# A sliding-window attention and SiLU feed-forward kernel: another order of loads, v of two batches by the hardware queue, attention half a tile further ahead

## The chip, the cores and the metric

The kernel runs on one core of a Trainium2 chip. A core has a matrix engine (PE, with its weight loads shown as PEld), a vector engine (DVE), a scalar engine with activation tables (ACT), a general engine (POOL) and a queue processor (SP); each works through its own instructions in the order in which they stand in the program, and they wait for each other by semaphores. Transfers are issued by SP (hardware queue) or POOL (software queue, which can change the type on the way) and run on 16 DMA engines. The metric is device time in microseconds, the median of three executions.

## The reference

```python
B, H, S, D = 8, 8, 576, 64                       # batch, heads, positions, head size
scores = q @ k.T / sqrt(D), kept where 0 <= i - j < 64
attn   = exp(scores - max) / (sum + 1e-9)
x      = (attn @ v), heads side by side          # 4608 tokens x 512
h      = x @ w_in                                # 512 x 2048
out    = (h * sigmoid(h)) @ w_out                # 2048 x 512
```

All inputs and the output are fp32; the kernel computes in bf16 with fp32 accumulation.

## The kernel before

**Blocks and tiles.** A batch has nine blocks of 64 positions; the 72 blocks run through all batches, and eight of them make a tile of 512 tokens, nine tiles in all. A block needs its own keys and the block before. The heads are worked on in two quads of four (a = 0, 1). For each quad of a group of blocks (`visit`): PE scores into four banks of PSUM (L339), ACT's exponential into `es` (L346), a multiplication with the mask on DVE (L353), PE values (L361) with a column of ones beside v for the sums, the reciprocal (L371) and the normalisation (L374) into `o` on DVE, and two DVE transposes (L380) into the tile's `xt`, of which there are three.

**Attention ahead.** Tile 0 is visited in groups of 3, 3 and 2 blocks as batch 0 arrives, tile 1 in two groups of four, and every later tile j + 1 as a whole, both quads, during the second layer of tile j, after its second product (`order[1]`).

**The two layers.** Tiles 0 and 1 run the first layer plain: 128x128 pieces of `w_in_sb` against 128 to 256 tokens (L388), and SiLU on ACT (L399) into `g`. Tile 0 runs the second layer plain too: 64 matmuls of 512 columns (L402). From tile 2 on the first layer, and from tile 1 on the second, use seven products in place of eight (`fast_first`, `fast_second`): 112 matmuls of 256 columns each (L438, L450). The sums of operands that this needs are made on DVE: `wsum1` and `wsum2` once, `xsum` from the tile's tokens (L411), `gsum` from the hidden activations (L407). Products are joined by copies of banks on ACT (L454) and additions on DVE (L457).

**Loads.** Batch 0 comes as fp32 by SP: k and q in thirds of 192 positions of a quad (`load_third`, L265) into memory that `gsum` and `wsum1` use later, v in four pieces and a half (L279, L276) into that of `wsum2`; casts (L291) and placements (`place_v`, L322) on ACT or DVE make bf16 of them. A piece of v needs three placements (`own`, `up`, `low`), as a block's values use a window of 128 positions that starts in the block before. POOL loads the rest with a change to bf16: w_in in eight pieces of 128 KB and four of 256 KB, batch 1 by thirds, w_out in eight pieces of 256 KB, the later batches by heads (`load_head`, L269). DVE transposes thirds with L298/L301 and heads with L308/L311, three operations each. `place_all` makes the `up` and `low` copies of the later batches on DVE (L327, L329).

**The order.** `Plan` simulates the engines with a cost for each operation, picks the ready operation with the lowest priority number, and writes the program in that order. Dependencies given to it decide its order alone; the waits in the program come from the data that instructions share. So an operation that the plan places late has no wait of its own unless it shares data with what it follows.

Of the kernel before, what the change touches and what calls it, by code (L numbers as in the profile page):

```python
# [31 lines left out]
class Plan:  # L32


    LATE = {"PE": 0.06, "ACT": 0.15, "DVE": 0.12, "POOL": 0.15, "SP": 0.0}
# [55 lines left out]
    def run(self):  # L91
# [3 lines left out]
        table, pipe = "exp", 0.0  # L95
# [7 lines left out]
        while left:  # L103
# [3 lines left out]
            while events and events[0] <= now + 1e-9:  # L107
                heapq.heappop(events)
            while self.returns and self.returns[0][0] <= now + 1e-9:
                _, _, b = heapq.heappop(self.returns)  # L110
                self.owner[b.idx], self.free_at[b.idx] = None, b.till
                if b.unit is not None:
                    b.unit.held -= 1
            moved = True
            while moved:
# [5 lines left out]
                for e in engines:  # L121
# [22 lines left out]
                    if op["dma"] is None:  # L144
                        op["seen"] = end + self.LATE[e]
                    else:
                        begin = max(pipe, end + 1.2)
                        pipe = begin + op["dma"]
                        op["seen"] = pipe + 2.0
# [4 lines left out]
                    for u, lat in op["users"]:  # L154
                        same = e in u["us"] and len(u["us"]) == 1 and op["dma"] is None
# [9 lines left out]
        self.order, self.span = order, max(op["seen"] for op in order)  # L165
# [5 lines left out]
def kernel(ctx, tc, q, k, v, w_in, w_out, out):  # L171
# [7 lines left out]
    NQ = 2  # L179
    NXT = 3  # L180
    NGP = 10
    scale = 1.0 / float(D) ** 0.5
# [18 lines left out]
    qT = [keep.tile([128, 6, 2, 96, 2], BF16, name=f"qT{a}") for a in range(NQ)]  # L201
# [71 lines left out]
    def load_v(e, b, g):  # L273
        if g == 4:
            dst = stage_v8 if b == 0 else vv[b % 2][64:128, :, 8, 0:D]
# [17 lines left out]
    def turn_third(b, a, kk, i):  # L293
# [5 lines left out]
        else:  # L299
            dst = qT[a][:, n].rearrange("x t y z -> x (t y z)").bitcast(FP32).rearrange("x (t p c) -> x c t p", t=2, c=3)  # L300
            nc.vector.transpose(out=dst, in_=src.rearrange("x (c t w) -> x c t w", c=3, t=2))  # L301

    def turn_blocks(b, a, kk, i):
        src = nats[b % 2][a][kk][:, 384 * i:384 * i + 384].bitcast(FP32).rearrange("x (n t w) -> x n t w", n=3, t=2)
        n = 3 * (b % 2) + i
        if kk:
            dst = kT[a][:, 64 + 192 * n:256 + 192 * n].rearrange("x t y -> x (t y)").bitcast(FP32)
            nc.vector.transpose(out=dst.rearrange("x (n p t) -> x n t p", n=3, t=2), in_=src)  # L308
        else:
            dst = qT[a][:, n].rearrange("x t y z -> x (t y z)").bitcast(FP32)  # L310
            nc.vector.transpose(out=dst.rearrange("x (t n p) -> x n t p", t=2, n=3), in_=src)  # L311

    def place_v(e, b, what, g):
# [5 lines left out]
        else:  # L319
            whole = stage_vp[:, g] if b == 0 else t[:, :, 2 * g + 1, 0:D]  # L320
# [12 lines left out]
    def scores(bank, a, blocks):  # L333
        for x, nb in enumerate(blocks):
            n, s = nb % 18, (nb % 18) * 64
            for par in range(2):
                for h in range(4):
# [4 lines left out]
                        rhs=qT[a][r, n // 3, :, 32 * (n % 3):32 * (n % 3) + 32, par],  # L342
# [34 lines left out]
    def turn_out(a, z, nb, n):  # L377
        src = osb[a][:, 0:n].rearrange("k n d t -> k n (d t)").bitcast(FP32)[:, :, 32 * z:32 * z + 32]
        j, s = nb // 8, nb % 8 * 64
        nc.vector.transpose(out=xts[j % NXT][:, 2 * a + z, s:s + 64 * n].bitcast(FP32), in_=src)  # L380
# [87 lines left out]
    SOFT = 0.85  # L468
# [4 lines left out]
    def turn_plan(b, a, kk, i, deps, prio, whole):  # L473
        old = score_ops.get((b - 2, a), []) + ([c_k] if kk and b == 0 and i == 0 else [])
        op = p.add({"DVE": dve(192)}, lambda _: (turn_third if whole else turn_blocks)(b, a, kk, i), deps + old, prio, tag="turn")
        turned.setdefault((b, a, i), []).append(op)
# [6 lines left out]
    n_soft = [0]  # L483

    def soft(us, fn, deps=(), dma=0.0, tag="load", after=()):
        n_soft[0] += 1
        return p.add({"POOL": us}, fn, deps, n_soft[0], dma=dma, tag=tag, after=after)
# [3 lines left out]
    def hard(fn, deps=(), dma=0.0, tag="load"):  # L491
# [3 lines left out]
    win, wout = {}, []  # L495

    def load_first(i):
        for a in range(NQ):
            for kk in (1, 0):
                ld = hard(lambda e, a=a, kk=kk: load_third(e, 0, a, kk, i), dma=0.52)  # L500
                ca = p.add({"ACT": act(384), "DVE": dve(384)}, lambda e, a=a, kk=kk: cast_third(e, a, kk, i), [ld], -50 + i, tag="cast")
                cast_ops.append(ca)
                turn_plan(0, a, kk, i, [ca], -50 + i, True)

    def load_first_v(g):
        ld = hard(lambda e: load_v(e, 0, g), dma=1.15 if g < 4 else 0.58)
        if g == 4:
            placed[(0, 8)] = [place_plan(0, "last", 4, [ld, c_v[0]], -30 + g)] + placed.get((0, 8), [])
            cast_ops.extend(placed[(0, 8)])
            return  # L510
        own, up, low = [place_plan(0, w, g, [ld, c_v[0]], -30 + g) for w in ("own", "up", "low")]
        cast_ops.extend((own, up, low))
        placed.setdefault((0, 2 * g + 1), []).append(own)
        placed.setdefault((0, 2 * g), []).append(up)
        placed.setdefault((0, 2 * g + 2), []).append(low)

    def load_rows(b, thirds, prio):
        for i in thirds:
            for a in range(NQ):
                for kk in (1, 0):  # L520
                    ld = soft(SOFT, lambda e, a=a, kk=kk, i=i: load_third(e, b, a, kk, i), turn_ops.get((b - 2, a, kk), []), dma=0.63)
                    turn_plan(b, a, kk, i, [ld], prio + 0.1 * i, True)

    def load_heads(b, prio):
        for a in range(NQ):
            for kk in (1, 0):
                ld = [soft(SOFT, lambda e, a=a, kk=kk, h=h: load_head(e, b, a, kk, h), turn_ops.get((b - 2, a, kk), []), dma=0.72)
                      for h in range(4)]
                for i in range(3):
# [347 lines left out]
```

## Time and profile before

| | |
|---|---|
| runs | 341.97, 342.42, 343.35 us; median 342.42 |
| profiled execution | 341.61 us; span of its instructions 339.9 us |
| mean granted clock of PE | 0.936 of full speed |
| busy, share of the span | PE 85%, PEld 67%, DVE 69%, ACT 61%, POOL 33% |
| DMA | 88061 packets, 30.25 MB: 16.63 MB by POOL's queue, 12.98 MB by SP's |
| matmuls | 4416 |

The profile shows one execution, in us from the start of the span. Its chain of waits is followed back from the last instruction, at each step to what released it or to the instruction before it on its engine. Groups give busy time, mean ns of one, then the idle time before them and what ended it. In a timeline row, the bracket is the engine's idle time before the row and its releaser. Where records overlap in time, as matmuls do, the time of a group is its covered time.

### The profile page before, as it was taken

The page shows a single profiled execution, that of the slowest core. Times are in us where ns is not written, and L with a number is a line of the kernel's source. Part 1 is how long each engine was busy: PE and PEld are TensorE (multiplying, and loading weights), DVE is VectorE, ACT ScalarE, POOL GpSimd, SP SyncE. Part 2 cuts the span into 40 slices and gives each one's busy share as a digit, 9 for nine tenths or more (in the row PEclk, how much of TensorE's full clock was granted, in tenths as well). Part 3 has the DMA queues.
Part 4 walks back from the last instruction along what each step waited for, and adds up shares of the span by engine and source line. Part 5 has one row for each costly group of instructions (what it writes and reads, how often), then busy time and mean ns, then how long its engine had stood idle before and what let it go on. Part 6 is the DMA issues. An engine that isn't in the chain of part 4 may idle for free.

```text
span 339.9 us, 10402 instructions
## 1 busy us (share of the span) xinstructions
PE 289.0 (85%) x4416; PEld 226.8 (67%) x4422; DVE 233.8 (69%) x603; ACT 208.8 (61%) x386; POOL 110.7 (33%) x170
## 2 busy tenths in 40 slices
PE   8374217999979679996999999999979989999994
PEld 3132206954758558884887788788858877887883
DVE  2132253859654798988598889969978686967840
ACT  2141627960985548863885797396659648866931
POOL 7041424597792457197009450300030000000000
PEclk9967556999999989998999999999999999999998
DMA  5988998999995399499209990560090030003003
GB/s 82 164 138 145 138 188 118 116 136 119 195 125 53 35 193 101 46 92 223 25 2 101 182 86 4 88 94 2 4 177 3 2 113 17 0 4 125 2 0 123
DMA packets 88061, 30.25 MB, mean 89 GB/s; under 512 B 76752, under 2 KB 82896, under 8 KB 88016
## 3 DMA queue, kind: packets, MB, share of 16 engines
q0 software_dynamic: 76848, 16.63, 53.5%
q1 hardware_dynamic: 11168, 12.98, 11.9%
q8 instruction: 34, 0.56, 0.7%
q14 instruction: 11, 0.09, 0.1%
HBM read 36.70 MB, written 9.44 MB: 136 GB/s over the span
## 4 chain that ended last, share of the span: by engine, by line
PE 46%; DVE 23%; SPq 11%; ACT 8%; DMA 5%; issue 4%; POOL 1%; DVEq 0%; ACTq 0%
PE bank L438 22%; PE bank L450 15%; SPq L265 7%; DVE o L374 5%; PE bank L388 5%; DMA wsum<-in_v_dram 4%; SPq L279 4%; DVE es L353 3%; PE bank L402 3%; DVE gsum L407 3%; DVE xt L380 2%; ACT es L346 2%; ACT L346 2%; PE bank L339 2%; DVE kT L308 1%
## 5 line engine op out<-in xcount | busy, mean ns | idle before, releaser
L450 PEld LDWEIGHTS <-gsum 128*128 128x128 bf16 x512 | 47.6, 98 | 11.1 <-DVE gsum L407 3.5
L460 ACT ACTIVATE g<-bank 128x512 bf16<-128x512 f32 x84 | 48.7, 617 | 4.6 <-PE bank L438 3.6
L438 PEld LDWEIGHTS <-wsum 128*128 128x128 bf16 x448 | 44.5, 99 | 10.5 <-issue 2.6
L450 PE MATMUL bank<-wsum,gsum 128*128 128x256 bf16 x384 | 47.3, 273 | 2.8 <-DVE gsum L407 2.0
L438 PE MATMUL bank<-xsum,wsum 128*128 128x256 bf16 x336 | 46.5, 279 | 1.2 <-DVE xsum L411 1.0
L279 POOL DMA_DIRECT2D vv<-in_v_dram x28 | 25.5, 930 | 58.6 <-PE bank L361 50.0
L346 ACT ACTIVATE es<-bank 128x512 bf16<-128x512 f32 (+3 forms) x96 | 39.5, 496 | 6.0 <-PE bank L339 5.9
L438 PEld LDWEIGHTS <-w_in_sb 128*128 128x128 bf16 x336 | 32.9, 99 | 13.8 <-issue 7.1
L450 PEld LDWEIGHTS <-g 128*128 128x128 bf16 x384 | 36.6, 98 | 7.2 <-issue 2.3
L269 POOL DMA_DIRECT2D nat<-in_k_dram x48 | 28.8, 614 | 36.7 <-DVE qT L311 30.9
L454 ACT COPY ot<-bank 128x512 f32<-128x512 f32 x23 | 13.4, 591 | 44.2 <-PE bank L450 29.8
L438 PE MATMUL bank<-xt,w_in_sb 128*128 128x256 bf16 x224 | 32.7, 281 | 6.5 <-DVE xt L380 3.6
L457 DVE TENSOR_TENSOR bank<-bank,part 128x512 f32<-128x512 f32 x36 | 24.5, 695 | 19.9 <-ACT part L454 10.3
L450 PE MATMUL bank<-w_out_sb,g 128*128 128x256 bf16 x256 | 33.9, 273 | 2.2 <-ACT bank L454 2.1
L407 DVE TENSOR_TENSOR gsum<-g 128x512 bf16<-128x512 bf16 x64 | 26.9, 421 | 11.2 <-ACT g L460 7.1
L388 PE MATMUL bank<-xt,w_in_sb 128*128 128x192 bf16 (+2 forms) x320 | 33.3, 266 | 0.6 <-ACT es L346 0.6
L353 DVE TENSOR_TENSOR es<-es,strip 128x1024 bf16<-128x1024 bf16 (+3 forms) x48 | 25.4, 546 | 11.5 <-ACT es L346 10.8
L269 POOL DMA_DIRECT2D nat<-in_q_dram x48 | 29.3, 627 | 12.1 <-DVE qT L311 10.1
L339 PE MATMUL bank<-qT,kT 32*128 32x64 bf16 x1152 | 14.3, 194 | 21.8 <-DVE qT L301 17.4
L388 PEld LDWEIGHTS <-w_in_sb 128*128 128x128 bf16 x320 | 28.5, 103 | 4.1 <-issue 1.5
L454 ACT COPY part<-bank 128x512 f32<-128x512 f32 x36 | 20.7, 594 | 16.4 <-PE bank L450 16.3
L374 DVE TENSOR_TENSOR o<-bank,rc 128x384 bf16<-128x384 f32 (+2 forms) x56 | 29.4, 527 | 1.9
(64 smaller groups left out, 435.2 us busy)
## 6 DMA issues: line engine op xcount, KB each, us to landing
out_dram<-ot SPq DMA_DIRECT2D x18, 512.0 KB
vv<-in_v_dram POOLq DMA_DIRECT2D x28, 128.0 KB, 4.0
nat<-in_k_dram POOLq DMA_DIRECT2D x48, 72.0 KB, 2.9
nat<-in_q_dram POOLq DMA_DIRECT2D x48, 72.0 KB, 3.0
w_out_sb<-in_moe_w_out_dram POOLq DMA_DIRECT2D x8, 256.0 KB, 14.0
wsum<-in_k_dram SPq DMA_DIRECT2D x6, 192.0 KB
gsum<-in_q_dram SPq DMA_DIRECT2D x6, 192.0 KB
w_in_sb<-in_moe_w_in_dram POOLq DMA_DIRECT2D x8, 128.0 KB, 16.2
```

The costliest lines, as they stand in the source:

```text
L269: queue[e].dma_start(out=nats[b % 2][a][kk][32 * h:32 * h + 32].rearrange("p (n x) -> p n x", n=NB), in_=(q, k)[kk][b, 4 * a + h].rearrang ...
L279: queue[e].dma_start(out=dst, in_=v[b, :, 128 * g:128 * g + 128].rearrange("h p d -> p h d"))
L346: nc.scalar.activation(out=es[a][:, h, 0:64 * n], in_=banks[bank.idx][:, 0:64 * n], func=ACTF.Exp, scale=scale)
L353: nc.vector.tensor_mul(t, t, strip[:, s:s + n].rearrange("k n i -> k (n i)").unsqueeze(1).to_broadcast([128, 2, 64 * n]))
L374: nc.vector.tensor_mul(osb[a][:, x0:x0 + n].rearrange("k n d t -> k n t d"), at_values(bank, n)[:, :, :, 0:D], rcs[w][:, 0:n].unsqueeze(3) ...
L388: nc.tensor.matmul(banks[bank.idx][:, i * n:i * n + n], lhsT=w_in_sb[:, c, 128 * ft:128 * ft + 128], rhs=xts[j % NXT][:, c, lo:hi], start= ...
L407: (nc.vector.tensor_sub if i else nc.vector.tensor_add)(out=dst[i], in0=a, in1=b)
L438: nc.tensor.matmul(banks[bank.idx][:, 256 * i:256 * i + 256], lhsT=lhs(z, i), rhs=rhs(z), start=(start and i == 0 and z == 0), stop=(z == ...
L450: nc.tensor.matmul(banks[bank.idx][:, 256 * m:256 * m + 256], lhsT=lhs(m, i), rhs=rhs(i), start=(start and i == 0 and m == 0), stop=(stop ...
L454: copies[e](out=dst, in_=src)
L457: nc.vector.tensor_add(out=dst, in0=bank, in1=part)
L460: nc.scalar.activation(out=g_tile(pair, 256 * t, 256 * t + 256), in_=src.rearrange("k (f t) -> k f t", f=2), func=ACTF.Silu)
```

## The change

It alters the planner's picture of DMA (two lanes, one per queue, that share time packet by packet), several of its costs, and:

- w_in comes in sixteen pieces of 128 KB, each given a dependency on the sixth load of SP (`GATE = 5`); POOL's first fifty loads are planned strictly one after the other;
- v of batch 1 comes by SP as fp32, like batch 0's (`HARDV = 2`), behind the eighth load of POOL in the plan (`VGATE = 7`) and behind the placements of batch 0 that free the memory; POOL issues w_out directly behind the first third of batch 1;
- batches 2 and 3 are loaded by thirds (`ROWS = 3`), and a batch loaded by heads is transposed in one operation for each of k and q of a quad, with `qT` laid out anew;
- the `up` and `low` copies of v of batch 2 and later run on ACT (`VACT = 2`);
- the two transposes into `xt` become one;
- `visit` takes one quad or both. During the second layer of tile j now come quad 1 of tile j + 1 and quad 0 of tile j + 2 (in tile 1: both quads of tile 2 and quad 0 of tile 3), behind the first product (`order[0]`) instead of the second;
- tile 1's second layer is plain, with its four groups of 128 tokens one after the other; the fast second layer begins with tile 2 (`F2 = 2`).

```diff
-        dst = stage_vp[:, g] if b == 0 else vv[b % 2][:, :, 2 * g + 1, 0:D]
+        dst = stage_vp[:, g] if b < HARDV else vv[b % 2][:, :, 2 * g + 1, 0:D]
...
-    def turn_blocks(b, a, kk, i):
-        src = nats[b % 2][a][kk][:, 384 * i:384 * i + 384].bitcast(FP32).rearrange("x (n t w) -> x n t w", n=3, t=2)
+    def turn_blocks(b, a, kk):
+        src = nats[b % 2][a][kk].bitcast(FP32).rearrange("x (n t w) -> x n t w", n=NB, t=2)
...
-    def turn_out(a, z, nb, n):
-        src = osb[a][:, 0:n].rearrange("k n d t -> k n (d t)").bitcast(FP32)[:, :, 32 * z:32 * z + 32]
+    def turn_out(a, nb, n):
+        src = osb[a][:, 0:n].rearrange("k n d t -> k n (d t)").bitcast(FP32).rearrange("k n (z w) -> k n z w", z=2)
         j, s = nb // 8, nb % 8 * 64
-        nc.vector.transpose(out=xts[j % NXT][:, 2 * a + z, s:s + 64 * n].bitcast(FP32), in_=src)
+        dst = xts[j % NXT][:, 2 * a:2 * a + 2, s:s + 64 * n].bitcast(FP32)
+        nc.vector.transpose(out=dst.rearrange("x z (n p) -> x n z p", n=n), in_=src)
...
+    def load_hard_v(b, g, deps=()):
+        ld = hard(lambda e: load_v(e, b, g), list(deps) + stage_free.get(g, []), dma=("h256", 1024 if g < 4 else 512))
+        first_loads.append(ld)
+        names = ("own", "up", "low") if g < 4 else ("last",)
+        ops = [place_plan(b, w, g, [ld, c_v[b % 2]], -30 + 50 * b + g) for w in names]
...
-        up = p.add({"DVE": dve(n, 3000)}, lambda e: place_all(e, b, "up", g0, g1), lv, prio, tag="place")
+        us = {"ACT": act(n)} if b >= VACT else {"DVE": dve(n, 3000)}
+        up = p.add(us, lambda e: place_all(e, b, "up", g0, g1), lv, prio, tag="place")
...
-        for f in range(16):
-            for m in range(4):
+        for f, m in [(f, m) for f in range(16) for m in range(4)] if j == 0 else [(f, m) for m in range(4) for f in range(16)]:
...
-                    cp = p.add({"ACT": act(512), "DVE": dve(512)}, lambda e, m=m: fork(e, ot[:, m], banks[bank[m].idx]), [op], base + 5, give=[bank[m]], tag="out")
+                    cp = p.add({"ACT": act(512), "DVE": dve(512)}, lambda e, m=m: fork(e, ot[:, m], banks[bank[m].idx]), [op] + ot_free.get((m // 2, 0), []), base + 5, give=[bank[m]], tag="out")
...
-    for pi0, pi1 in ((0, 2), (2, 4), (4, 8)):
+    for pi0, pi1 in ((0, 2), (2, 4), (4, 6), (6, 8)):
         for c in range(4):
-            ld = soft(SOFT, lambda e, c=c, pi0=pi0, pi1=pi1: load_w_in(e, c, 256 * pi0, 256 * pi1), dma=0.39 * (pi1 - pi0))
+            ld = soft(SOFT, lambda e, c=c, pi0=pi0, pi1=pi1: load_w_in(e, c, 256 * pi0, 256 * pi1), [first_loads[GATE]], dma=("s1024", 64 * (pi1 - pi0)))
...
     load_rows(1, (0,), 20)
-    load_pairs(1, (0, 1))
+    for g in range(5):
+        load_hard_v(1, g, [soft_last[VGATE]])
...
+            if n_b[0] <= ROWS:
+                load_rows(n_b[0], (0, 1, 2), 100 * j - 80)
+            else:
+                load_heads(n_b[0], 100 * j - 80)
...
-        order = fast_second(j, j == NT - 1)
-        if j + 1 < NT:
-            visit(list(range(8 * j + 8, 8 * j + 16)), 100 * j + 52, after=[order[1]], sprio=100 * j + 50.0)
+        order = fast_second(j, j == NT - 1) if j >= F2 else plain_second(j)
+        todo = [(j + 1, 0)] * (j == 1) + [(j + 1, 1), (j + 2, 0)]
+        for i, (t, a) in enumerate(todo):
+            if t < NT:
+                load_until(8 * t + 7, j)
+                visit(list(range(8 * t, 8 * t + 8)), 100 * j + 52 + i, after=[order[0]], sprio=100 * j + 50.0 + 0.1 * i, quads=(a,))
```

More of the change, by code (lines that the diff above doesn't have):

```diff
@@ L164, in run @@
                     heapq.heappush(events, end)
-        self.order, self.span = order, max(op["seen"] for op in order)
+            next_flow()
+        self.order, self.span = order, max(op["seen"] or 0.0 for op in order)
         for op in order:
@@ L555, with visit @@
     n_val = [0]
-    def visit(blocks, prio, after=(), sprio=None):
+    def visit(blocks, prio, after=(), sprio=None, quads=(0, 1)):
         n, j = len(blocks), blocks[0] // 8
         exps, outs = [], []
-        for a in range(NQ):
-            bank = [Bank("start") for _ in range(4)]
+        for a in quads:
+            bank = [Bank("start" if n == 8 else "part") for _ in range(4)]
             need = []
@@ L566, in visit @@
                         need += turned[(x // NB, a, x % NB // 3)]
-            sc = p.add({"PE": 0.1 + 0.12 * n}, lambda _, bank=bank, a=a: scores(bank, a, blocks), need, prio + 0.01 * a if sprio is None else sprio + 0.01 * a,
+            sc = p.add({"PE": 0.1 + 0.08 * n}, lambda _, bank=bank, a=a: scores(bank, a, blocks), need, prio + 0.01 * a if sprio is None else sprio + 0.01 * a,
                        take=bank, after=after, tag="scores")
@@ L583, in visit @@
                     need = need + placed[divmod(nb, NB)]
-                va = p.add({"PE": 0.1 + 0.1 * m}, lambda _, vb=vb, a=a, part=part, x0=x0: values(vb, a, part, x0), need, (prio if sprio is None else sprio) + 0.01 * a + 0.001 * x0,
+                va = p.add({"PE": 0.1 + 0.105 * m}, lambda _, vb=vb, a=a, part=part, x0=x0: values(vb, a, part, x0), need, (prio if sprio is None else sprio) + 0.01 * a + 0.001 * x0,
                            take=[vb], tag="values")
@@ L625, in plain_first @@
                 fts = [2 * pi + i for pi in pairs for i in range(2)]
-                bank = Bank("start")
+                bank = Bank("start" if 2 * size * n == 512 else "part")
                 need = []
```

178 lines of the change are left out of this document (112 added, 66 removed).

## The prediction

> **What bounds the kernel now.** I read the page's head and its 40 slices first, then the busy time by stage, then the chain of waits, then the timeline where the chain leaves TensorE.
>
> ```profile
> span 339.9 us, 10402 instructions
> PE   8374217999979679996999999999979989999994
> PEclk9967556999999989998999999999999999999998
> DMA  5988998999995399499209990560090030003003
> ```
>
> Three parts. Until slice 7 (60 us) PE is mostly idle and the DMA engines are full: loading sets the pace, and PE's granted clock sinks to half. Then a mixed stretch, then PE at 9 nearly throughout. The stretches, cut where PE begins tile 0's second layer (69.4), ends it (85.6), begins the second half of tile 1's first layer (100.9), and begins each later tile:
>
> ```profile
> core 0: us, PE busy (x) PEld busy (x) DVE busy (x) ACT busy (x) POOL busy (x), PEclk, DMA share, GB/s
> 0.00:69.40 69.40, 39.98 (x501) 26.46 (x505) 27.53 (x88) 31.33 (x69) 27.77 (x46) 0.75 0.91 135
> 85.60:100.90 15.30, 13.02 (x225) 10.31 (x224) 9.47 (x30) 14.67 (x25) 13.12 (x23) 1.00 1.24 168
> 100.90:125.40 24.50, 19.58 (x402) 16.14 (x401) 18.29 (x49) 11.95 (x20) 9.12 (x15) 1.00 0.74 95
> 125.40:159.70 34.30, 31.40 (x489) 25.16 (x489) 30.70 (x79) 22.59 (x41) 23.71 (x38) 0.95 1.04 110
> 159.70:190.70 31.00, 30.47 (x481) 24.75 (x481) 24.47 (x60) 21.98 (x40) 10.00 (x14) 0.94 0.65 63
> 190.70:220.80 30.10, 29.05 (x485) 24.41 (x485) 27.36 (x71) 22.25 (x41) 9.91 (x14) 1.00 0.61 83
> 220.80:251.80 31.00, 29.11 (x481) 23.87 (x481) 26.55 (x66) 21.42 (x39) 3.32 (x4) 1.00 0.37 67
> 251.80:282.20 30.40, 28.75 (x480) 23.78 (x480) 23.45 (x54) 21.33 (x39) 0.00 (x0) 1.00 0.25 46
> 282.20:311.40 29.20, 28.36 (x480) 23.98 (x480) 22.01 (x52) 21.15 (x39) 0.00 (x0) 1.00 0.07 26
> 311.40:339.90 28.50, 23.57 (x212) 20.53 (x211) 12.83 (x28) 15.27 (x28) 0.00 (x0) 0.95 0.13 50
> ```
>
> From 125.4 on six tiles take 34.3, 31.0, 30.1, 31.0, 30.4 and 29.2, together 186.0 us. What do they lose? The chain of waits and the timeline at one tile's end:
>
> ```profile
> 276.89 1.19 DVE es L353 x2
> 278.77 0.58 DVE o L374
> 280.62 0.77 DVE xt L380 x2
> 281.74 0.44 DVE xsum L411
> 311.41 9.96 PE bank L438 x88
> 323.63 11.37 PE bank L450 x104
> ```
>
> ```profile
> 268.06 0.68 PE L339 MATMUL bank<-qT,kT 32*128 32x64 bf16 x64
> 272.99 0.72 PE L361 MATMUL bank<-vv,es 128*32 128x65 bf16 x64
> 279.40 1.29 PE L438 MATMUL bank<-xt,w_in_sb 128*128 128x256 bf16 x8 [0.58 <-DVE o L374]
> 282.21 1.91 PE L438 MATMUL bank<-xsum,wsum 128*128 128x256 bf16 x16 [0.28 <-DVE xsum L411]
> ```
>
> The mask, normalisation, transposition and token sums of the second quad of heads run on DVE from 276.9 to 282.2, and PE, which has finished the second layer, waits for them in pieces. PE's own work in a tile is 224 matmuls at 9.96/88 = 0.113 us, 25.4 us, and two quads of attention at 0.68 + 0.72, 2.8 us: 28.2. Six tiles need 169.2, so 16.8 us can be won there.
>
> **The change part by part.**
>
> *The front (to 69.4).* "Held back" is a dependency inside the planner alone. In the changed program the first eight w_in loads on POOL wait on no semaphore, as before, and SP's first sixteen loads stand in the same order. So I expect no hold.
>
> ```profile
> 1.52 5.58 POOL L284 DMA_DIRECT2D w_in_sb<-in_moe_w_in_dram  x8
> 37.78 1.42 POOL L287 DMA_DIRECT2D w_out_sb<-in_moe_w_out_dram  x2 [0.43 <-DMA w_in_sb<-in_moe_w_in_dram]
> 25.62 0.51 ACT L291 CAST nat<-wsum 128x384 bf16<-128x384 f32 x1 [0.64 <-DMA wsum<-in_k_dram]
> 29.78 0.51 ACT L291 CAST nat<-gsum 128x384 bf16<-128x384 f32 x1 [3.65 <-DMA gsum<-in_q_dram]
> 34.88 0.51 ACT L291 CAST nat<-wsum 128x384 bf16<-128x384 f32 x1 [4.59 <-DMA wsum<-in_k_dram]
> 47.41 0.51 ACT L291 CAST nat<-wsum 128x384 bf16<-128x384 f32 x1 [4.71 <-DMA wsum<-in_k_dram]
> 49.60 0.36 DVE L291 CAST nat<-gsum 128x384 bf16<-128x384 f32 x1 [2.56 <-DMA gsum<-in_q_dram]
> 52.80 1.90 ACT L322 CAST vv<-wsum 128x512 bf16<-128x512 f32 x3 [3.54 <-DMA wsum<-in_v_dram]
> 59.26 1.28 ACT L399 ACT_TABLE_LOAD   x1
> 60.44 9.03 PE L388 MATMUL bank<-xt,w_in_sb 128*128 128x192 bf16 x128
> ```
>
> The casts mark when batch 0's thirds land: the last q third at 49.6, the last big v piece at 52.8. The new ACT order puts casts of later thirds ahead of exponentials, so first-layer groups that PE ran in gaps before 58 now come in one run of 176 matmuls after 16 early ones. It can start when the last scores are done, at about 53 (49.6, two table loads, 2.6, and some 0.8 for a transposition and a first exponential). 128 matmuls took 9.03; by the mean, 0.07 each, 176 take 12.4; I add 1.4 for two quads' values (0.72 each, above) and 2 for a start at half clock (the slices before 57 us show 5 and 6): 68.8, against 69.4. I take 0. The bounds: -4.9, if w_in in 128 KB pieces lets the k/q loads from 25.6 on land 2.19 us apart (47.41 to 49.60) instead of 4.63 (25.62 to 34.88, two steps): 2 x 2.44; and +9.8, if w_out, now issued ahead of v, spreads the four last thirds in the same way: 4 x 2.44.
>
> [...]
>
> *Tile 1.* Between tile 0's second layer and the last exponentials of tile 1, ACT is the bound: 14.67 busy of 15.3.
>
> ```profile
> 76.72 9.02 PE L402 MATMUL bank<-w_out_sb,g 128*128 128x512 bf16 x40
> 98.56 0.60 PE L450 MATMUL bank<-w_out_sb,g 128*128 128x256 bf16 x4 [2.09 <-ACT bank L454]
> 100.92 7.24 PE L388 MATMUL bank<-xt,w_in_sb 128*128 128x256 bf16 x64
> 113.09 1.05 PE L450 MATMUL bank<-wsum,gsum 128*128 128x256 bf16 x8 [1.97 <-DVE gsum L407]
> L322 ACT CAST vv<-wsum 64x512 bf16<-64x512 f32 x7 | 4.3, 617 | 2.1 <-DMA wsum<-in_v_dram 1.8
> ```
>
> v of batch 1 now comes as fp32 and needs 13 placements on ACT and DVE; five stand on ACT in this stretch: 5 x 0.617 = 3.1 us, so the second half of the first layer starts at 100.9 + 3.1 = 104.0. The fast second layer filled PE meanwhile with 32 matmuls that need the first 256 tokens alone; the plain one can't, and PE waits some 9 us. Then 7.2 (as before), 64 plain matmuls at 9.02/40 = 0.2255, 14.4, attention of tile 2, 2.8, and of the first quad of tile 3 the scores and 24 of 64 value matmuls, 0.68 + 0.27 = 0.95. That reaches 129.4. The waits for gsum and the fork (1.97, 2.09) and 16 DVE sums go, but they lie inside 125.4, which this sum replaces.
>
> The wait itself has a price. In 125.4:159.7 the clock is 0.95: 5% of 34.3, 1.7 us, followed a wait of PE at the start of tile 2; in 85.6:100.9, with 2.09 us idle, it stayed 1.00. By rows, between 0 and 1.7. [...] I take 1.7 by the row. The stage ends at 131.1: +5.7, between +3 (no dip, placements done before the output copies) and +9 (two dips more).
>
> *Tiles 2 to 8.* Scores now follow the first product of the second layer: quad 1 of the next tile, then quad 0 of the tile after. In the changed PE order m5, m4 and m3 (48 matmuls) follow the last values that the next tile needs, at 0.109 each (11.37/104), 5.2 us; the DVE work behind them (278.77 to 282.2 in the chain above, 3.4 us, and a reciprocal) fits under that. Of the 16.8 us I leave 0.8 per tile for what ACT and DVE still delay: 16.8 - 4.8 = 12.0, and 0.95 of tile 3's attention has moved to tile 1: -12.95. Bounds: -17.7 (all of it) and -5.
>
> *At nothing:* two transposes to xt become one (0.77 for two now), three of k or q become one, and v's up and low copies move from DVE to ACT. A 2048-wide ACT copy isn't in the trace; between 4 x 0.617 and 0.617, and I take 1.8 by its length: 3.6 a batch. ACT is busy 21.3 of 30.4 us; with 3.2 more per tile, 24.5 of 29. Without that slack it costs up to 3.2 per tile. Batches 2 and 3 by thirds: POOL is idle two thirds of the time from 159.7 on. The new wait of tile 1's output copies on tile 0's store finds it issued some 25 us earlier (85.6 against 111); behind it stand only ACT's next copies.
>
> Sum: 0 + 5.7 - 12.95 = -7.25. The profiled execution (span 339.9) took 341.61 us and the median of the runs is 342.42; I take the difference from the median: 335.2.
>
> **The rivals.**
> - *Quicker front.* Smaller w_in pieces bring the k/q thirds 4.9 us earlier: 330.3. For it: the 4.63 us spacing while 256 KB pieces were under way. [...]
> - *DVE and ACT take the gain.* DVE is busy 27.36 of 30.1 and 26.55 of 31.0 us, and ACT gains 3.2 per tile; if their in-order queues hold forks and joins back, the tiles give 5 instead of 12.95: 343.1. Against: DVE's six tiles sum to 154.5, under 169.2.
> - *Slower: w_out on the path of tile 0.* From 34 us on the software queue carries w_out instead of v. If its packets share the engines with the last four thirds as w_in's did, each takes 4.63 us: front +9.8, total +2.55, 345.0, and more if the tiles fall short too. It decides once the thirds that were cast at 47.4 and 49.6 come 4 us apart or more. Against: two w_out pieces were queued at 37.8 already, and these thirds came 2.19 apart.
> - *The change doesn't do what it says:* that w_in isn't held is part of the forecast.
>
> **How the numbers follow.** Forecast 0.52, quicker front 0.12, DVE and ACT 0.18, slower 0.18. The range takes in the quicker front with the tiles' bound (330.3 - 4.75, 326) and the slow one: 326 to 345; the forecast's own is 331 to 339. Changes under 0.5% (340.7 to 344.1) can't be told from none: faster 0.67 (the first two cases and a quarter of the third), same 0.15, slower 0.18.
>
> **What would show it.** w_in's first loads still issued at 1.5 us, and the last v of batch 0 cast at 52 to 55; PE's closed first-layer run ending at 67 to 71; a gap of PE of 6 to 9 us before the second half of tile 1's first layer, with a granted clock of 0.5 behind it; the first L438 of the fast layers (L487 in the changed kernel) at 129 to 133; then tiles 28.5 to 29.5 us apart without a wait for xt or xsum. Wrong it is if batch 0 lands 5 us or more earlier or later, or if a tile still takes 30 us.

## The result and the profile after

| | before | changed |
|---|---|---|
| median of the runs | 342.27 us | 338.52 us (336.24 to 338.63) |
| changed / before | | 0.987, 95% interval 0.982 to 0.992 |
| span of the profiled execution | 339.9 us | 336.8 us |
| busy DVE, ACT | 233.8, 208.8 us | 216.1, 234.4 us |

The change made the kernel 3.75 us faster by the medians of four executions each, about half of the 7.2 us that were forecast. One of the twelve executions of `f2one_vdve` below was slow (347.46 us) and is left out of its median. The first view of the changed kernel is its 40 slices.

```profile
span 336.8 us, 10253 instructions
PE   8173587999739999989999999998997999999994
PEclk9757569999967999999999999999999799999999
```

Two slices of PE's clock stand out behind the front: the low stretch around slice 11 (95 us), and a 7 in slice 31 (260 us). The stretches of the changed kernel, cut at the same events (tile 0's second layer begins at 66.5 and ends at 82.3, the second half of tile 1's first layer begins at 100.1, the first fast product stands at 128.0, later tiles follow):

```profile
core 0: us, PE busy (x) PEld busy (x) DVE busy (x) ACT busy (x) POOL busy (x), PEclk, DMA share, GB/s
0.00:66.50 66.50, 43.09 (x538) 25.97 (x542) 20.67 (x64) 30.21 (x70) 25.75 (x43) 0.77 0.88 147
82.30:100.10 17.80, 10.49 (x195) 8.18 (x193) 12.59 (x36) 17.13 (x28) 8.58 (x13) 0.86 1.12 160
100.10:128.00 27.90, 26.80 (x463) 16.66 (x470) 23.13 (x64) 16.83 (x26) 13.85 (x21) 0.90 0.84 85
128.00:158.20 30.20, 28.55 (x457) 23.80 (x457) 24.68 (x55) 25.57 (x41) 25.80 (x41) 1.00 1.28 126
158.20:187.40 29.20, 28.95 (x483) 23.72 (x481) 23.62 (x52) 25.06 (x40) 13.11 (x19) 1.00 0.84 94
187.40:217.20 29.80, 28.85 (x483) 24.22 (x481) 23.69 (x52) 24.97 (x40) 3.31 (x4) 1.00 0.26 48
217.20:247.10 29.90, 28.85 (x483) 24.06 (x481) 26.04 (x56) 25.48 (x41) 3.31 (x4) 1.00 0.50 63
247.10:280.60 33.50, 30.86 (x547) 25.30 (x545) 21.89 (x50) 26.24 (x42) 0.00 (x0) 0.95 0.12 43
280.60:307.40 26.80, 26.65 (x358) 22.84 (x353) 19.85 (x45) 19.36 (x35) 0.00 (x0) 1.00 0.08 29
```

From PE's timeline I take four terms for every kernel below: the front (until tile 0's second layer begins), the middle (to the first fast product of tile 2), the tiles (to PE's last matmul), and the rest of the span.

| profiled execution, us | front | middle | tiles | rest |
|---|---|---|---|---|
| before | 69.8 | 55.7 | 209.6 | 4.9 |
| changed | 66.5 | 61.5 | 204.4 | 4.3 |
| difference | -3.3 | +5.9 | -5.1 | -0.6 |

Each row of terms is one execution. The kernels `changed`, `copies_last`, `copies_dve` and `fill_last` below run the same program up to the end of the front and show 66.1 to 67.9 us for it, so a difference of a term under 2 us is not shown by such a row alone.

The tile that begins at 247.1 takes 33.5 us, 3.3 to 4.3 more than the four before it; 64 more matmuls of attention are some 0.7 of that. The timeline of ACT and PE there shows why (start, duration, engine and line; the bracket is the idle time before and its releaser):

```profile
256.56 1.90 ACT L375 COPY vv<-vv 64x2048 bf16<-64x2048 bf16 x1
258.22 0.54 PE L409 MATMUL bank<-vv,es 128*32 128x65 bf16 x16
258.49 1.90 ACT L377 COPY vv<-vv 64x2048 bf16<-64x2048 bf16 x1
260.30 0.58 ACT L503 COPY bank<-bank 128x512 f32<-128x512 f32 x1
260.82 0.58 ACT L503 COPY part<-bank 128x512 f32<-128x512 f32 x1
260.93 0.60 PE L487 MATMUL bank<-xsum,wsum 128*128 128x256 bf16 x4 [2.17 <-ACT bank L503]
262.38 0.90 PE L487 MATMUL bank<-xsum,wsum 128*128 128x256 bf16 x4 [0.42 <-DVE bank L506]
263.08 1.06 PE L487 MATMUL bank<-xsum,w_in_sb 128*128 128x256 bf16 x4
```

The `up` and `low` copies of v of batch 7 stand in ACT's queue ahead of the two copies of banks that PE waits for. PE stops for 2.17 us, and four matmuls that take 0.60 us at full clock take 1.06 at 263.08, with the granted clock at 0.50 from 262.5 to 265.9: the half clock follows the wait. Before the change these copies were DVE's, and cheap there; the groups of the two kernels (busy time, mean ns of one):

```profile
L327 DVE COPY vv<-vv 64x2048 bf16<-64x2048 bf16 (+1 forms) x8 | 5.4, 674 | 0.2
```
```profile
L375 ACT COPY vv<-vv 64x2048 bf16<-64x2048 bf16 x6 | 11.4, 1905 | 0.1
L377 ACT COPY vv<-vv 64x2048 bf16<-64x2048 bf16 x6 | 11.4, 1905 | 0.1
```

Twelve copies of 1.905 us are 22.9 us of ACT's time. On DVE, in the kernel before, the median copy took 689 ns (the mean of 674 takes in two shorter copies), 1.2 us less than on ACT.

In the front, POOL issues the thirds of batch 1 (`nat` from `in_k`) only at 31.4 us, and the last thirds of batch 0 are cast earlier, at 32.2 in place of 34.9 and 47.8 in place of 49.6:

```profile
25.98 0.67 POOL L332 DMA_DIRECT2D w_in_sb<-in_moe_w_in_dram  x1 [1.52 <-DMA w_in_sb<-in_moe_w_in_dram]
31.38 0.67 POOL L313 DMA_DIRECT2D nat<-in_k_dram  x1 [4.73 <-DMA w_in_sb<-in_moe_w_in_dram]
```
```profile
32.22 0.51 ACT L339 CAST nat<-wsum 128x384 bf16<-128x384 f32 x1 [3.72 <-DMA wsum<-in_k_dram]
40.59 0.51 ACT L339 CAST nat<-wsum 128x384 bf16<-128x384 f32 x1 [2.23 <-DMA wsum<-in_k_dram]
42.79 0.51 ACT L339 CAST nat<-gsum 128x384 bf16<-128x384 f32 x1 [1.02 <-DMA gsum<-in_q_dram]
44.95 0.51 ACT L339 CAST nat<-wsum 128x384 bf16<-128x384 f32 x1 [0.75 <-DMA wsum<-in_k_dram]
47.78 0.51 ACT L339 CAST nat<-gsum 128x384 bf16<-128x384 f32 x1 [1.59 <-DMA gsum<-in_q_dram]
```

### The profile page after: what moved, and what is told of

Same layout as the page of the kernel before. It is cut to its first block, busy times and chain, and to the rows that moved or that the text cites. A ratio compares the mean times of both kernels' runs of the same rounds, so it can differ in the third digit from the quotient of the medians.

```text
span 336.8 us, 10253 instructions
## 1 busy us (share of the span) xinstructions
PE 293.5 (87%) x4367; PEld 223.6 (66%) x4381; DVE 216.1 (64%) x514; ACT 234.4 (70%) x407; POOL 105.4 (31%) x161
## 5 line engine op out<-in xcount | busy, mean ns | idle before, releaser
L499 PEld LDWEIGHTS <-gsum 128*128 128x128 bf16 x448 | 42.7, 98 | 6.8 <-DVE gsum L456 1.1
L401 DVE TENSOR_TENSOR es<-es,strip 128x1024 bf16<-128x1024 bf16 (+3 forms) x48 | 25.6, 550 | 32.3 <-ACT es L394 31.8
L499 PE MATMUL bank<-wsum,gsum 128*128 128x256 bf16 x336 | 40.3, 273 | 1.0 <-DVE gsum L456 0.8
L327 POOL DMA_DIRECT2D vv<-in_v_dram x24 | 21.3, 903 | 55.3 <-PE bank L409 52.0
L499 PEld LDWEIGHTS <-g 128*128 128x128 bf16 x336 | 32.2, 99 | 5.5 <-ACT g L509 1.0
L437 PE MATMUL bank<-xt,w_in_sb 128*128 128x256 bf16 (+2 forms) x320 | 33.2, 265 | 3.0 <-DVE xt L429 2.0
L499 PE MATMUL bank<-w_out_sb,g 128*128 128x256 bf16 x224 | 30.5, 276 | 0.7 <-ACT g L509 0.7
L387 PEld LDWEIGHTS <-kT 32*128 32x128 bf16 x1152 | 12.1, 94 | 27.5 <-issue 20.2
L317 POOL DMA_DIRECT2D nat<-in_k_dram x32 | 19.4, 626 | 32.2 <-DVE qT L349 16.4
L451 PE MATMUL bank<-w_out_sb,g 128*128 128x512 bf16 x118 | 27.7, 379 | 1.1 <-issue 1.0
L456 DVE TENSOR_TENSOR gsum<-g 128x512 bf16<-128x512 bf16 x56 | 23.4, 417 | 5.2 <-ACT g L509 4.9
## 6 DMA issues: line engine op xcount, KB each, us to landing
vv<-in_v_dram POOLq DMA_DIRECT2D x24, 128.0 KB, 4.6
w_in_sb<-in_moe_w_in_dram POOLq DMA_DIRECT2D x16, 128.0 KB, 17.3
```

Of the source, the lines that this page charges most:

```text
L327: queue[e].dma_start(out=dst, in_=v[b, :, 128 * g:128 * g + 128].rearrange("h p d -> p h d"))
L387: nc.tensor.matmul(banks[bank[h].idx][:, 64 * x:64 * x + 64].rearrange("k (t p) -> k t p", t=2), lhsT=kT[a][r, s:s + 128, par], rhs=qT[a][ ...
L401: nc.vector.tensor_mul(t, t, strip[:, s:s + n].rearrange("k n i -> k (n i)").unsqueeze(1).to_broadcast([128, 2, 64 * n]))
L437: nc.tensor.matmul(banks[bank.idx][:, i * n:i * n + n], lhsT=w_in_sb[:, c, 128 * ft:128 * ft + 128], rhs=xts[j % NXT][:, c, lo:hi], start= ...
L451: nc.tensor.matmul(banks[bank.idx], lhsT=gall[:, pair, f % 2, 128 * m:128 * m + 128], rhs=w_out_sb[:, f], start=(f == 0), stop=(f == 15))
L456: (nc.vector.tensor_sub if i else nc.vector.tensor_add)(out=dst[i], in0=a, in1=b)
```

## The experiments

Times are medians; the ratio is to the kernel before in the same comparison, with its 95% interval.

| kernel | median us | ratio | front, middle, tiles |
|---|---|---|---|
| changed | 338.52 | 0.987 (0.982 to 0.992) | 66.5, 61.5, 204.4 |
| copies_last | 335.58 | 0.981 (0.977 to 0.984) | 66.4, 60.8, 201.9 |
| copies_dve | 335.89 | 0.982 (0.979 to 0.985) | 67.9, 61.2, 201.7 |
| fill_last | 335.80 | 0.982 (0.978 to 0.985) | 66.1, 60.2, 201.9 |
| win256 | 341.19 | 0.995 (0.993 to 0.998) | 68.7, 60.8, 204.1 |
| b_win128 (from before) | 340.16 | 0.994 (0.991 to 0.997) | 68.5, 56.6, 208.7 |
| vdve | 341.10 | 0.997 (0.994 to 1.000) | 67.0, 60.7, 207.3 |
| softv_vdve | 335.63 | 0.982 (0.980 to 0.985) | 69.0, 55.4, 202.3 |
| softv_copies | 338.19 | 0.989 (0.986 to 0.993) | 70.7, 56.9, 206.5 |
| f2one_vdve | 343.01 | 1.003 (1.001 to 1.006) | 66.2, 54.5, 216.3 |
| nohalf_vdve | 339.75 | 0.994 (0.992 to 0.996) | 68.2, 61.3, 205.3 |
| nohalf_copies | 347.67 | 1.017 (1.013 to 1.020) | 66.4, 61.3, 213.8 |
| nohalf | 356.08 | 1.043 (1.040 to 1.046) | 66.8, 60.7, 221.0 |

**The copies of v on ACT.** `copies_last` and `copies_dve` leave the plan and every other instruction as they are and issue the copies on DVE, for batch 7 alone and for all six batches.

```diff
-        t = vv[b % 2]
+        t, e = vv[b % 2], "DVE" if b == 7 else e          # copies_dve: b >= VACT
```

> The changed kernel with the up and low copies of v of batch 7 alone on DVE instead of ACT; every other instruction stays in its place on its engine. Theory A: the two 1.90 us copies on ACT at 256.6 and 258.5 us hold back the copies of banks that PE waits for (2.17 us, then 0.42), and the half clock of 262.5 to 265.9 (some 1.7 us lost) follows from that wait. Then both go: 4.3 us less, about 334.2. Rival B: the clock drops anyway, or the clock's part is no loss: 2.2 to 2.6 us less, about 336.1. Rival C: PE would stop at that place in any case, since the transposition into xt and the normalisation of the same quad end at 260.3: under 1 us less, 337.5 to 338.5.

> The changed kernel with the up and low copies of v of batches 2 to 7 on DVE, twelve copies of about 0.69 us there (as in the kernel before) in place of twelve of 1.905 us on ACT; the order of everything else is kept. Theory A: the copies on ACT also cause the small waits of PE in the tiles that begin at 128.0 and 217.2 (0.78, 0.44, 0.75 us for gsum and banks), so this gains 1 to 2 us on top of the run with batch 7 alone: about 333. Rival B: only batch 7's copies matter: the same as that run within 0.5 us. Rival C: DVE, which then carries 8.3 us more, holds the joins and the masks back: 1 us or more slower than the run with batch 7 alone.

Two copies out of twelve are worth 2.9 us (338.52 to 335.58), and 2.5 us in the tiles. That lies between theories A (4.3) and B (2.2 to 2.6). The half clock at 262.5 is gone, but PE now waits 0.63 and 1.21 us for DVE at the same place, which A had not reckoned with:

```profile
257.15 0.60 PE L487 MATMUL bank<-xt,wsum 128*128 128x256 bf16 x4 [0.63 <-DVE fin L506]
260.60 0.60 PE L487 MATMUL bank<-xsum,wsum 128*128 128x256 bf16 x4 [1.21 <-DVE bank L506]
261.04 0.60 PE L487 MATMUL bank<-xsum,w_in_sb 128*128 128x256 bf16 x4
```

Moving the other ten copies adds nothing in sum (335.89): rival B of `copies_dve`. Tile by tile it is a trade: against `copies_last` the tile from 216.4 gets 1.3 us shorter (29.9 to 28.5), the first two get 1.4 us longer (59.4 to 60.8), and PE waits 2.0 us once for `gsum`, made on DVE, where it waited 0.8.

**The size of w_in's pieces.** `win256` loads the second half of w_in in four pieces of 256 KB again, `b_win128` splits these four in the kernel before; in both the order of all engines but POOL is the same as in its base.

```diff
-load_w_in(e, c, 256 * pi0, 256 * pi1)
+load_w_in(e, c, 256 * pi0, 256 * (8 if pi0 == 4 else pi1)) if pi0 < 6 else None                # win256
+[load_w_in(e, c, 256 * x, 256 * x + 512) for x in range(pi0, pi1, 2)]                           # b_win128, from before
```

> The changed kernel with the last eight pieces of w_in as four of 256 KB, as before the change; everything else in its order. Theory A: the smaller pieces are what brought batch 0's thirds forward (last q third cast 2 to 2.5 us earlier than before): then the last thirds and the last v piece land 2 to 2.5 us later, PE ends tile 0's first layer at 68 to 69 instead of 66.2, and the time rises by 2 to 3 us, to about 341. Rival B: the front's gain has another source (the order of casts on ACT and of PE's first-layer groups): the landings and the time stay within 0.7 us of the changed kernel's, 338 to 339.

> The kernel before with the four 256 KB pieces of w_in split into eight of 128 KB at the same place of POOL's queue; nothing else changed. Theory A (small pieces bring the thirds forward): batch 0's last third and v land about 2 us earlier; PE's closed first-layer run, which began at 60.4, begins 1.5 to 2 us earlier; time 340.3 to 341. Rival B: no difference in the landings: 342.0 to 342.7.

Theory A twice: 2.7 us slower with the large pieces, 2.2 us faster with the small ones (by the fronts of one execution each, 2.2 and 1.3). In `win256` POOL issues batch 1's thirds 9.5 us earlier than in the changed kernel, and batch 0's later thirds land 2.3 to 2.5 us later:

```profile
21.92 0.67 POOL L313 DMA_DIRECT2D nat<-in_k_dram  x1 [2.35 <-DMA w_in_sb<-in_moe_w_in_dram]
22.66 0.76 POOL L313 DMA_DIRECT2D nat<-in_q_dram  x1
```
```profile
34.70 0.51 ACT L339 CAST nat<-wsum 128x384 bf16<-128x384 f32 x1 [4.14 <-DMA wsum<-in_k_dram]
50.03 0.51 ACT L339 CAST nat<-gsum 128x384 bf16<-128x384 f32 x1 [1.79 <-DMA gsum<-in_q_dram]
```

POOL issues eight w_in pieces at once, by 7.1 us in the changed kernel, and each further issue waits until a piece has landed (the bracket; the ninth is issued at 13.16 us, after 6.04 us of waiting). In the traces of the kernel before and the changed one these loads count on eight semaphores in turn, and the ninth load waits on that of the first, so the limit of eight is the program's. So the size of a piece sets how much the software queue has under way here: small pieces hold back what POOL issues next. That the share of the engines is what the thirds gain is the reading that fits; it was not measured by itself.

**Parts of the plan.** The next runs change a setting and let the plan order everything anew, from `vdve`, which plans the copies of v on DVE:

```diff
-    SOFT, ROWS, VACT, F1, F2 = 0.69, 3, 2, 2, 2
+    SOFT, ROWS, VACT, F1, F2 = 0.69, 3, 9, 2, 2        # vdve;  f2one_vdve: F2 = 1 as well
-    HARDV = 2
+    HARDV = 1                                          # softv: with load_pairs and place_pairs of batch 1 as before
-        todo = [(j + 1, 0)] * (j == 1) + [(j + 1, 1), (j + 2, 0)]
+        todo = [(j + 1, 0), (j + 1, 1)]                # nohalf: with after=[order[1]]
```

> The changed kernel with VACT = 9: the up and low copies of v of all later batches are planned and run on DVE, so the plan's order also changes; it is the base for the next three. Theory A: the plan that knows of the copies on DVE is as good as the one that had them on ACT with the copies moved by hand: 335 to 336.5. Rival B: with the copies where the plan can weigh them it also takes away the small waits left in tiles 2, 5 and 6 (0.6 to 1.2 us each): 333 to 334.5. Rival C: DVE's longer queue delays masks and joins: 337 or more.

> As vdve, but tile 1's second layer is the fast one again (F2 = 1). Theory A: the plain layer's longer PE work and PE's wait with nothing to do ahead of tile 1's last exponentials are its price, 5.7 us by the forecast, so the fast one, which fills that wait with 32 matmuls, gains 3 to 5 us. Rival B: the fast layer brings back the waits for gsum and for the fork that the kernel before had there (1.97 and 2.09 us) and its 28 DVE sums and joins delay tile 2: within 1 us of vdve, or slower.

> As vdve, but v of batch 1 by POOL's queue with a change of type, as in the kernel before, and its up and low copies on DVE (HARDV = 1). Theory A: five placements of 0.63 us leave ACT's queue ahead of tile 1's exponentials, and PE's wait before the second half of tile 1's first layer shrinks by about 3 us: 2 to 4 us less than vdve. Rival B: the loads of v on POOL (128-byte pieces) share the engines with batch 0's last thirds and delay w_out and batch 1's thirds, so that the front gives back 1 to 2 us or tile 1 waits for its data: within 1 us of vdve.

> The base is copies_dve (335.89 us). Here v of batch 1 comes by POOL's queue in bf16 again (HARDV = 1), so that no placements of it stand on ACT. Theory A: as between vdve and softv_vdve, the stretch from tile 0's second layer to the first fast product shrinks by some 5 us (60.7 to 55.4 there) and the front gives 1 to 2 us back: 332 to 333. Rival B: the gain there was vdve's own half clock at 185.5 and the waits around it, and the shorter stretch is eaten by the later front: 335 to 336.5.

`vdve` is 5.2 us slower than `copies_dve`, with the same work on the same engines but for two output copies: rival C. PE waits 2.3 us for `xt` and 1.8 us for the normalisation in its tiles (its view of PE's waits), and a half clock of 6.8 us follows the wait of 1.39 us at 183.9 (four matmuls take 0.60 us at 183.29 and 1.01 at 189.28). So a new plan moves the time by some 5 us through order, and a single run with a new plan can't price a part.

With that in mind: the fast second layer of tile 1 is not better (343.01, 1.9 us above `vdve`, rival B). The first fast product comes 7 us earlier, but PE waits for masks, `xt` and joins in and ahead of tile 2, and in this stretch of 29 us it has half clock for 17:

```profile
100.00:129.00 29.00, 21.32 (x440) 15.85 (x440) 24.49 (x63) 15.49 (x27) 14.73 (x23) 0.70 0.76 64
```

v of batch 1 on POOL's queue shortens the middle by 5.3 us (`softv_vdve`) and 4.3 us (`softv_copies`) and lengthens the front by 2.0 and 2.8, so in these two pairs of executions that part of the change costs 1.5 to 3.3 us before the tiles. The totals differ by their tiles: 5.5 us faster than `vdve`, more than theory A said, and 2.3 slower than `copies_dve`, where neither theory held. In `softv_copies` PE waits 1.07 us for a copy of v that stands on DVE where the plan had ACT, and 2.0 us for a normalisation behind it, and a half clock of 6.8 us begins there: three matmuls at 150.51 take 0.82 us, where three at 142.83 took 0.49.

**Attention half a tile ahead.**

> As vdve, but attention runs as in the kernel before: during the second layer of tile j, after its second product, both quads of tile j + 1 and nothing of tile j + 2. Theory A (the forecast's): attention half a tile further ahead is what removes the waits for xt and xsum at the tiles' ends, 0.8 to 2.2 us at each of six, and the half clock behind the longest two: without it the tiles take 7 to 10 us more, 342 to 345. Rival B: in the steady tiles it gains only what PE idled there, 0.3 to 0.6 us each, and the half clocks at the start of tiles 2 and 3 come from the stage ahead of them: 1 to 4 us more than vdve.

> The base is copies_dve (335.89 us): the changed kernel's plan with the up and low copies of v moved by hand to DVE. Here attention runs as before the change (both quads of tile j + 1 during the second layer of tile j, after its second product). Theory A (the forecast's): attention half a tile further ahead is worth most of what the tiles gained: 7 us or more above the base, 343. Rival B (from nohalf_vdve, whose tiles took 205.3 us with waits of 0.7 us at their ends and no half clock): it is worth 0.3 to 0.6 us per tile, 2 to 4 us in all: 338 to 340. Rival C: nothing, 336, as nohalf_vdve against vdve seems to say.

> The changed kernel (338.52 us) with attention as before the change and nothing else undone: both quads of tile j + 1 during the second layer of tile j, after its second product; the copies of v stay on ACT. Theory A: attention half a tile further ahead carries the gain of the tiles, and without it they take 7 us or more longer than the changed kernel's 204.4 from the first fast product to PE's end: 345 and more. Rival B: the steady tiles lose 0.3 to 0.8 us each, as in nohalf_vdve (205.3): 339 to 341.5. Rival C: nohalf_copies' 347.67 comes from the copies by hand, whose place on DVE lies ahead of masks and sums that PE waits for at the tiles' ends; with them on ACT no such wait, and 338 to 340, with waits of 0.6 to 0.7 us for xt and banks at every tile's end.

The three undo the same part under three placements of the copies of v. The tiles' time, in us:

| attention | copies on ACT | on DVE by hand | planned on DVE |
|---|---|---|---|
| half a tile further ahead | 204.4 (changed) | 201.7 (copies_dve) | 207.3 (vdve) |
| as before | 221.0 (nohalf) | 213.8 (nohalf_copies) | 205.3 (nohalf_vdve) |

With the copies on ACT, undoing the part takes the tiles 16.6 us more, more than twice the least that theory A of `nohalf` named, and its rivals B and C fall. `nohalf_copies` is 11.8 us slower than its base, its theory A by the time. `nohalf_vdve` is 1.4 us faster than its base, and neither of its theories held. PE's waits in `nohalf` (who waited for whom, total us, times, longest) and a stretch of its timeline show what happens:

```profile
PE bank L499 <- ACT g L509: 4.5, 3, 1.7
PE bank L487 <- ACT bank L503: 3.8, 6, 0.7
PE bank L409 <- DVE es L401: 3.1, 6, 1.4
PE bank L499 <- ACT bank L503: 2.8, 2, 1.8
PE bank L487 <- DVE o L422: 2.5, 4, 0.7
```
```profile
238.03 1.91 ACT L377 COPY vv<-vv 64x2048 bf16<-64x2048 bf16 x1
239.84 0.59 ACT L509 ACTIVATE g<-bank 128x512 bf16<-128x512 f32 x1
242.11 0.61 PE L499 MATMUL bank<-w_out_sb,g 128*128 128x256 bf16 x4 [1.70 <-ACT g L509]
```

The copies now delay SiLU, and PE waits for `g`; a half clock follows twice. `nohalf` and `nohalf_copies` have one plan, so the copies on ACT alone cost 8.4 us there (356.08 and 347.67), where all twelve cost 2.6 in the changed kernel: with the attention further ahead, the same copies on ACT hold up less. That is some 6 us of the part's 16.6. The rest is not priced. `nohalf_copies` and `nohalf_vdve` do the same work but for the plan, and lie 7.9 us apart; so the 12.1 us between the tiles of `copies_dve` and `nohalf_copies` may be the plan as well as the part. In all three kernels without the part PE waits 2.5 or 2.6 us for `o`, as it never does in the changed one; but `vdve`, which has the part, waits 4.1 for `xt` and `o`. In the tiles of `nohalf_vdve`, without copies on ACT, PE idles 1.0 to 1.9 us each, about as before the change (0.9 to 1.7 from the third fast tile on).

**The price of the half clock.** `fill_last` is `copies_last` with twenty matmuls on zeros where PE waits in tile 1.

```diff
+    def fills(bank, n):
+        for _ in range(n):
+            nc.tensor.matmul(banks[bank.idx][:, 0:512], lhsT=fill[:, 0:128], rhs=fill, start=True, stop=True)
...
+        fills(bank[0], 6 if blocks[0] == 12 and a == 1 else 0)                # scores
+        fills(bank, 10 if blocks[0] == 12 and a == 1 else 0)                  # values
+        fills(bank, 4 if j == 1 and lo == 256 and fts[0] == 0 else 0)         # first_plain
```

> The base is copies_last (335.58 us). Twenty matmuls on zeros, which add nothing to the result, stand in PE's queue where it waits in tile 1: 6 ahead of the last scores, 10 ahead of the last values, 4 ahead of the second half of the first layer; the banks they write are overwritten by the work that follows. Theory A: the half clock of 93.7 to 103.9 us follows from PE's waits there (6.5 us of 9) and goes; the 62 matmuls behind it take 7.2 instead of 9.5 us, and the time falls by 1.5 to 2.5 us, to 333 to 334. Rival B: the clock falls all the same, or the fills push back the work that they stand ahead of by as much as they save: 335 to 336.5. Rival C: they delay the exponentials' banks, 337 or more.

Rows of `copies_last` and of `fill_last` at the second half of tile 1's first layer, and the stretch of `fill_last` ahead of it:

```profile
100.04 8.81 PE L437 MATMUL bank<-xt,w_in_sb 128*128 128x256 bf16 x62 [1.13 <-DVE xt L429]
```
```profile
96.17 2.32 PE L383 MATMUL bank<-fill 128*128 128x512 bf16 x10 [2.27 <-ACT es L399]
100.61 6.93 PE L444 MATMUL bank<-xt,w_in_sb 128*128 128x256 bf16 x62 [0.58 <-DVE xt L435]
```
```profile
90.50:100.00 9.50, 5.93 (x100) 2.99 (x94) 8.21 (x24) 8.75 (x14) 2.01 (x3) 1.00 0.86 105
```

The clock stays at 1.00 (0.67 in the same stretch of `copies_last`) and the 62 matmuls take 1.9 us less, as theory A has it: the half clock follows the wait and can be kept away. But the ten fills had to wait for their bank (2.27 us, released by ACT), ran into the time of the last values, and the second half began 0.6 us later. The first fast product comes 0.9 us earlier in this execution (126.3 against 127.2), but the median is the same, 335.80: by the time, rival B.

No run beats `copies_last`; it, `softv_vdve` (335.63), `fill_last` (335.80) and `copies_dve` (335.89) can't be told apart, and their medians lie 2.6 to 2.9 us under the changed kernel's.

## Why the prediction was right and where it was not

The time fell inside the range (326 to 345) and inside the forecast's own (331 to 339), but the sum of 0 + 5.7 - 12.95 came out as -3.3 + 5.9 - 5.1 and -0.6 at the end: two terms were mis-sized, with opposite signs. That the total stayed in the forecast's own range is luck to that extent: the front gave 3.3 us that were not forecast, and the tiles 7.8 less than forecast. By the prediction's own sign, a tile that still takes 30 us, the tiles' term was wrong: the tile from 128.0 takes 30.2, that from 247.1 takes 33.5. (And its chance of faster, as it words it, adds up to 0.69 in place of 0.67.)

- *The front, forecast 0.* That POOL's first pieces wait for nothing held. What failed is the chance of 0.12 for the quicker front, an estimate of mine: the piece size alone is worth 2.2 to 2.7 us of the kernel's time, as `win256` and `b_win128` show from both sides; where the rest of the 3.3 comes from was not separated. POOL's own waits stood in the quoted profile: "0.43 <-DMA w_in_sb" before w_out says that POOL issues no more than a number of transfers ahead, and I did not ask what a smaller piece does to that. PE's closed run ended at 66.2, below the 67 that was named as its sign. The casts showed the room: the last third came at 49.6 us, and those at 25.6, 29.8 and 34.9 were 4.6 apart on average, where the last two came 2.2 apart.
- *The slower rival (w_out ahead of v).* It did not come: the last thirds land 2.2 to 2.8 us apart, where 4 was its mark.
- *Tile 1, forecast +5.7.* Measured +5.9. ACT's five placements and the wait of PE came as worked out: the second half began 33.6 us after tile 0's second layer, against 31.2 before (100.92 - 69.75), where 3.1 more was forecast. So that step gave 2.4, not 3.1. The clock's price, put at 1.7, is 2.6: the 62 matmuls of the second half took 9.56 us here and 6.93 in `fill_last`. That the wait has a price was the step that carried this term; its two misses, 0.7 and 0.9, cancel by luck.
```profile
100.10 9.56 PE L437 MATMUL bank<-xt,w_in_sb 128*128 128x256 bf16 x62 [1.13 <-DVE xt L429]
```
- *Tiles 2 to 8, forecast -12.95, measured -5.1.* The mechanism is there: the two half clocks (0.95 and 0.94 in the tiles before) are gone from the tiles at 128.0 and 158.2, and PE's waits for `xt`, `o` and `xsum`, 6.5 us in the tiles before, are gone from its list of waits. PE's rows from the first fast product to its last matmul, before and after, give the sizes:
```profile
125.41:334.98 209.57, 200.69 (x3104) 166.48 (x3103) 167.37 (x404) 145.41 (x260) 46.92 (x69) 0.98 0.46 62
128.03:332.46 204.43, 197.77 (x3016) 165.73 (x3015) 152.12 (x332) 163.10 (x268) 45.52 (x68) 0.99 0.46 65
```
PE's idle time fell from 8.9 to 6.7 us, two half clocks of 3.41 us (some 1.7 each) became one, and 88 matmuls of tile 3 moved ahead of the tiles, 0.95: together 4.9 of the 5.1. What failed is the base of the sum, "16.8 us can be won there". Idle time and half clocks were 12.3 us in all, 4.5 less. PE's own work in six tiles is 171.0 us, 28.5 each (the sum row of the six full tiles of `nohalf_vdve`, below), where I used 28.2, from a stretch of one line alone; that is 1.8 us. And the cut at 311.4 lies 2.1 us behind the last tile's first product, at 309.3. Then, of what could be won, 8.4 us were left (6.7 idle and one half clock), where 4.8 had been put. The largest part of that is the copies of v on ACT, "at nothing, 21.3 busy of 30.4". ACT had the room on average, and five of six batches cost nothing in sum; the sixth landed in front of a join and cost 2.5 us in the tiles. I had the duration nearly right (1.8 against 1.905) and gave the price of the cover gone, up to 3.2 per tile; what was missing is the question of which instructions stand behind the copy in the queue.
```profile
sum 179.60, PE 170.96 PEld 143.31 DVE 146.45 ACT 128.89 POOL 42.79; mean PE 28.49 PEld 23.89 DVE 24.41 ACT 21.48 POOL 7.13
```

- *The rival "DVE and ACT take the gain"* gave the tiles 5 us; they gave 5.1. The figure agrees, the reason only in part: a queue that holds joins back (ACT's) took 2.5 of the 7.8 us that were missing, and 4.5 were never there. I had forecast each case with everything else at its likeliest and no case with both.

What stays open: how much of the tiles' gain each part carries, since the parts' worths depend on each other (the table of attention and copies) and a new plan moves several us by itself; and what ended the half clocks of tiles 2 and 3. They are gone in `nohalf_copies` and `nohalf_vdve` too, without attention half a tile ahead and with the copies of v on DVE, so neither is needed for it. DVE's shorter transposes and tile 1's plain second layer remain; in `f2one_vdve`, with the fast one, a half clock of 17 us lies over the start of tile 2 again, though under a new plan.

## What to carry to other kernels

A copy that an engine has room for on average still has a place in its queue: name what stands behind it, and find the places where PE waits for that engine (here 2.17 us behind two copies of 1.9 us). When a program lets a queue have a fixed number of transfers under way, the size of one transfer decides how early the next tensor's loads begin (here at 31.4 us with pieces of 128 KB, at 21.9 with the last ones of 256 KB). In a kernel whose order a planner writes, price a part by keeping the plan and moving only that part; a new plan moved this one by 5 and by 8 us with nearly the same work.

## What the hardware showed that I had not expected

I had reckoned with a half clock behind the 9 us of tile 1; it also followed far shorter waits. In the kernel before, waits of 1.34 and 0.74 us end at 123.90 and 125.41, and the clock is at half from 125.6 to 129.0; waits of 2.21 and 0.27 us end at 158.16 and 159.68, and it is at half from 159.7 to 163.1. In the changed kernel waits of 2.17 and 0.42 us end at 260.93 and 262.38, and it is at half from 262.5 to 265.9. Each of these three lasts 3.41 us; the half clock in tile 1 of the changed kernel, where PE waits 3.12 and then 1.13 us, lasts 10.24 (95.3 to 105.5). Waits were not always followed by it: behind one of 2.09 us that ends at 98.56 in the kernel before, and behind 0.63 and 1.21 us in `copies_last` (ending at 257.15 and 260.60), the clock stayed at 1.00. So the length of a single wait does not settle it here. (A few matmul records are missing from a trace, and their ends are modelled, so the waits are rough.) And matmuls on zeros in place of waits kept the clock up: with 18 recorded fills, that of `fill_last` is 1.00 from 90.5 to 109.7 us, where that of `copies_last` is 0.67 in the first half of this stretch and 0.80 in the second.
